# Issuing the loads of x in pieces of three chunks, nine chunks in flight

## The chip, the cores and the metric

One NeuronCore of one Trainium2 chip. TensorE (PE, with its weight loads as PEld), VectorE (DVE), ScalarE (ACT), GpSimd (POOL) and SyncE (SP) each work through a list of instructions of their own; 16 DMA engines move data. The metric is the device time of one execution in microseconds (us), the median of several runs. The kernel before takes 177.07 us, the median of 3 runs from 176.68 to 177.59.

## The reference

x is 8 batches of 4224 tokens of 192 numbers, in float32. It goes through a causal convolution over 7 tokens whose weights are softmax-normalised, one set for each of 8 groups of 24 channels, and the result y through token mixing:

```
w   = softmax(weight, axis=-1)                       # 8 x 7
y   = sum over k of w[h, k] * x_padded[b, s + k, h]  # per group h of 24 channels
wq, wk = y @ w_q, y @ w_k                            # 192 -> 64
W   = (wq @ wk.T) / 8                                # 4224 x 4224, never formed here
out = relu(W @ y) @ w_out
```

The kernel uses (wq @ wk.T) @ y = wq @ (w_k.T @ (y.T @ y)): a Gram matrix y.T @ y of 192 x 192 for each batch, a small matrix M made of it, and then wq @ M for all tokens, relu, and the product with w_out.

## The kernel before

**Tiles.** Tokens are cut into chunks of 122 (CW); with the 6 tokens before them a chunk fills the 128 partitions. A batch has NCC = 35 chunks. XW (line 355) holds all chunks of all 8 batches as bfloat16, so no load of x ever waits for a buffer. The convolution of a group of channels is a product of XW with a banded matrix BAND, line 654.

**Groups.** A batch's chunks are loaded and convolved by groups: four of 9, 9, 9 and 8 chunks in batch 0, two of 18 and 17 chunks in the others (groups_of, line 314).

**Loads.** gen_load (line 535) makes the loads of one group, issued on POOL, which turns float32 into bfloat16 on the way: the first chunk of a batch by itself (it has no tokens before it), all full chunks of the group in one DMA, and the last chunk by itself (82 rows). A batch after batch 0 has four DMAs: 1 and 17 chunks, 16 and 1 chunks. All DMAs of a group count on one semaphore of its own, and the group's convolutions (gen_conv, line 636) wait for it. POOL has nothing else to do after a few microseconds, and no load of x waits for an earlier one. The SP queue issues the loads of the weights and, line 978, the stores of the output, from four buffers (NOUT).

**Stages of a batch.** After a group's convolution (lines 391 and 392 are the helper that records each pair of matmuls) ACT or DVE writes y to SBUF (line 671). PE transposes y (lines 395, 396 and 726) and multiplies it with w_q (lines 751 and 755), and adds up the Gram matrix (line 787). From it come M (lines 806 to 860), the mixing (lines 878 and 890), relu (lines 907 and 908), the product with w_out (line 935 and the helper at 391 and 392), its copy to the output buffer (line 970) and the store. The mixing of a batch is interleaved with the convolutions, transposes and Gram matmuls of the next.

**The order.** Each operation is an Op with an estimated duration, the operations it needs, and a priority vt. Planner.plan (line 143) places them one by one on the engines, by readiness and then by vt, and so writes each engine's list before anything runs. The priorities are read one after another from the list TURNS (line 13), one entry for each operation in the order in which they are made:

```
op.vt = TURNS[len(planner.ops)]
```

For a load the planner does not use the time at which its issue ends alone but a due time, `op.lands`, which counts 260 ns for each chunk loaded so far. Program.place (line 232) then turns each operation's needs into semaphore waits. A wait is left out where the engine, or the clock of another operation waited for, already vouches for it:

```
for source in list(waits):
    if any(s != source and waits[s][2].get(source, 0) >= waits[source][0] for s in waits):
        del waits[source]
```

A wait that an instruction doesn't carry itself is an instruction of its own on the engine (line 269).

Of the kernel before, what the change touches and what calls it, by code (L numbers as in the profile page):

```python
# [12 lines left out]
TURNS = [  # L13
    int(t) / 1000
    for t in """
# [56 lines left out]
class Op:  # L72


    n = 0
# [199 lines left out]


Op.dma = None


def bass_lightweight_conv__then__hypermixer_token_mlp_kernel(  # L280
# [8 lines left out]
    B, S, D = x.shape  # L289
    H, KC = weight.shape  # L290
# [5 lines left out]
    x_t, out_t, w_t = x.tensor, out.tensor, weight.tensor  # L296
    wq_t, wk_t, wo_t = moe_w_q.tensor, moe_w_k.tensor, moe_w_out.tensor

    CW = 128 - (KC - 1)
# [7 lines left out]
    while t < S:  # L307
        n = 512 if S - t >= 1024 else 128
# [5 lines left out]
    def groups_of(b):  # L314
        size = 9 if b == 0 else 18
        return [list(range(c, min(c + size, NCC))) for c in range(0, NCC, size)]
# [4 lines left out]
    def sbuf(name, shape, dtype):  # L321
        return es.enter_context(nc.sbuf_tensor(name, shape, dtype))

    def semaphore(name):
        return es.enter_context(nc.semaphore(name))
# [29 lines left out]
    XW = sbuf("xw", [128, B, NCC, D], BF16)  # L355
# [16 lines left out]
    planner = Planner(nbank=7, first_bank=0)  # L372
# [1 line left out]
    def bank(i, n=1):  # L374
        return PS[:, i * 512 : (i + n) * 512]

    def add(*a, dma=None, kind=None, **k):
        op = Op(*a, **k)
        op.dma = dma
        op.kind = kind  # L380
        op.vt = TURNS[len(planner.ops)]
        return planner.add(op)

    def evac_ns(cols, fast=1):
# [9 lines left out]
    def turn_halves(e, out, in_, identity):  # L394
# [3 lines left out]

    S_W = semaphore("s_w")
    load_w = add(  # L400
        "SP",
        lambda e, op: e.dma_start(WT_F[:, :, :], bass.AP(w_t, 0, [[0, 128], [1, H * KC]])),
        100,
        dma=("w", S_W, 16),
        tail=2500,
        vt=-9,
    )

    one = add("DVE", lambda e, op: e.memset(IDENT[:, :], 1.0), 100, vt=-9.5)
    zero_w = add("DVE", lambda e, op: e.memset(WQT[64:128, :, wq_cols[-2] :], 0.0), 150, vt=-8.51)  # L410
    zero_yt = add("DVE", lambda e, op: e.memset(YTH[64:128, wq_cols[-2] :], 0.0), 100, vt=-8.52)
    zero_s = add("DVE", lambda e, op: e.memset(STEPT[:, :], 0.0), 150, vt=-8.9)
# [18 lines left out]
        vt=-9,  # L431
# [99 lines left out]

    load = {}
    at = [5000.0]

    def gen_load(b, gi):
        sem = semaphore(f"s_x{b}_{gi}")
        cs = groups_of(b)[gi]
        parts = []
        base = b * S * D
        full = [c for c in cs if 0 < c < NCC - 1]  # L540
        if cs[0] == 0:
            parts.append((XW[KC - 1 : 128, b, 0, :], bass.AP(x_t, base, [[D, CW], [1, D]])))
        n = len(full)
        parts.append(
            (
                XW[:, b, full[0] : full[0] + n, :],
                bass.AP(x_t, base + (CW * full[0] - KC + 1) * D, [[D, 128], [CW * D, n], [1, D]]),
            )
        )
        if cs[-1] == NCC - 1:  # L550
            rows = S - (CW * (NCC - 1) - KC + 1)
            parts.append(
                (
                    XW[0:rows, b, NCC - 1, :],
                    bass.AP(x_t, base + (CW * (NCC - 1) - KC + 1) * D, [[D, rows], [1, D]]),
                )
            )

        at[0] += len(cs) * 260.0
        load[b, gi] = []  # L560
        for k, part in enumerate(parts):
            first = (b, gi) == (0, 0) and part[0].shape[1] > 1 and len(part[0].shape) == 3
            op = add(
                "POOL",
                lambda e, op, part=part: e.dma_start(*part),  # L565
                900,
                needs=[zero_x] if cs[-1] == NCC - 1 else [],
                after=[] if first else [ident],
                dma=(f"x{b}_{gi}", sem, 16),
                vt=-10 if first else -4 + b + gi * 0.1 + 0.02 * k,  # L570
            )
            op.tail = 1500.0
            op.lands = at[0]
            load[b, gi].append(op)

    for gi in range(len(groups_of(0))):
        gen_load(0, gi)
# [40 lines left out]
    for b in range(1, B):  # L618
        for gi in range(len(groups_of(b))):
            gen_load(b, gi)  # L620
# [386 lines left out]
        later = nxt  # L1007

    planner.plan()

    program = Program(semaphore)
    for op in planner.order:
# [46 lines left out]
```

## Time and profile before

| what | us |
|---|---|
| median of 3 runs | 177.07 |
| the profiled execution: span from its first to its last instruction | 175.7 |
| PE busy | 157.1 |
| ACT busy | 123.5 |
| DVE busy | 118.0 |
| POOL busy | 30.3 |

The profiled execution is a run of its own; its span lies 1.4 us below the median of the runs. In the view of the DMA queues, q0 are the loads that POOL issues, q1 those and the stores that SP issues, and q8 the engines' instructions. The sizes there are those of the written side: a chunk of x is 48 KB as bfloat16 and twice that as it is read. In the windows, each engine has its busy time and in brackets its number of instructions, then come the granted TensorE clock as a share, the DMA engines' share (over 1 where transfers overlap) and GB/s.

Where in the span the loads and the convolutions stood, from the issue and landing rows of the loads and the timeline of PE:

| batch and group | last load of the group landed, us | its first convolution, us |
|---|---|---|
| 1, first | 21.3 | 23.5 |
| 1, second | 25.6 | 28.6 |
| 2, first | 30.2 | 34.4 |
| 2, second | 34.5 | 37.8 |
| 3, first | 39.1 | 47.7 |
| 3, second | 45.5 | 54.4 |
| 7, second | 106.0 | 134.0 |

### The profile page before, as it was taken

The page shows a single profiled execution, that of the slowest core. Times are in us where ns is not written, and L with a number is a line of the kernel's source. Part 1 is how long each engine was busy: PE and PEld are TensorE (multiplying, and loading weights), DVE is VectorE, ACT ScalarE, POOL GpSimd, SP SyncE. Part 2 cuts the span into 40 slices and gives each one's busy share as a digit, 9 for nine tenths or more (in the row PEclk, how much of TensorE's full clock was granted, in tenths as well). Part 3 has the DMA queues.
Part 4 walks back from the last instruction along what each step waited for, and adds up shares of the span by engine and source line. Part 5 has one row for each costly group of instructions (what it writes and reads, how often), then busy time and mean ns, then how long its engine had stood idle before and what let it go on. Part 6 is the DMA issues. An engine that isn't in the chain of part 4 may idle for free.

```text
span 175.7 us, 7099 instructions
## 1 busy us (share of the span) xinstructions
PE 157.1 (89%) x3226; PEld 121.7 (69%) x3226; DVE 118.0 (67%) x216; ACT 123.5 (70%) x206; POOL 30.3 (17%) x39
## 2 busy tenths in 40 slices
PE   0289799888999999899989979999999999999990
PEld 0179666776787787668778766878767777877550
DVE  6556587765766677586787738689688675765740
ACT  3243677597787948668648747888888896698980
POOL 7999452524230000000000000000000000000000
PEclk9999999999999999999999999999999999999995
DMA  3999999999999999999999999067283045987787
GB/s 30 162 189 186 205 191 193 191 196 277 193 279 194 286 309 268 343 250 243 304 264 282 237 194 348 24 244 297 103 343 127 4 175 216 356 347 309 265 303 262
DMA packets 48157, 40.36 MB, mean 230 GB/s; under 512 B 37632, under 2 KB 40960, under 8 KB 48128
## 3 DMA queue, kind: packets, MB, share of 16 engines
q0 software_dynamic: 36128, 13.61, 65.1%
q1 hardware_dynamic: 12000, 26.31, 40.9%
q8 instruction: 25, 0.41, 0.9%
q14 instruction: 4, 0.03, 0.1%
HBM read 27.56 MB, written 25.95 MB: 305 GB/s over the span
## 4 chain that ended last, share of the span: by engine, by line
PE 88%; issue 4%; DVE 3%; ACT 2%
PE ps L391 25%; PE ps L787 14%; PE ps L935 8%; PE ps L392 7%; PE ps L395 6%; PE ps L726 6%; PE ps L878 5%; PE ps L751 4%; PE ps L890 4%; PE ps L755 4%; PE ps L396 3%; ACT rt L907 1%; ACT out_sb L970 1%; DVE band L527 0%; DVE xw L416 0%
## 5 line engine op out<-in xcount | busy, mean ns | idle before, releaser
L970 ACT COPY out_sb<-ps 128x768 f32<-128x768 f32 (+1 forms) x46 | 34.7, 768 | 15.1 <-PE ps L392 11.3
L671 ACT CAST y<-ps 122x816 bf16<-122x816 f32 (+3 forms) x46 | 35.7, 791 | 13.2 <-PE ps L392 12.8
L907 ACT ACTIVATE rt<-ps 128x1024 bf16<-128x1024 f32 (+3 forms) x44 | 34.1, 800 | 6.4 <-PE ps L878 4.5
L787 PE MATMUL ps<-y 122*64 122x192 bf16 (+4 forms) x840 | 33.8, 222 | 2.2 <-issue 2.2
L970 DVE COPY out_sb<-ps 128x768 f32<-128x768 f32 (+1 forms) x26 | 21.6, 840 | 19.7 <-PE ps L392 18.5
L392 PE MATMUL ps<-wol,rt 128*64 128x192 bf16 x264 | 33.9, 255 | 1.0 <-issue 1.0
L787 PEld LDWEIGHTS ps<-y 122*64 122x64 bf16 (+1 forms) x840 | 31.1, 112 | 4.9 <-issue 2.8
L565 POOL DMA_DIRECT2D xw<-in_x_dram x34 | 29.9, 893 | 22.3 <-issue 21.5
L391 PE MATMUL ps<-wol,rt 128*64 128x192 bf16 x264 | 33.7, 255 | 0.0
L391 PE MATMUL ps<-xw,band 128*64 128x432 bf16 (+3 forms) x144 | 31.8, 335 | 1.5 <-DVE band L527 0.9
L392 PE MATMUL ps<-xw,band 128*64 128x432 bf16 (+3 forms) x144 | 32.1, 337 | 1.1 <-issue 1.1
L391 PEld LDWEIGHTS ps<-wol,rt 128*64 128x64 bf16 x264 | 24.1, 138 | 8.1 <-issue 2.0
L908 DVE TENSOR_SCALAR rt<-ps 128x512 bf16<-128x512 f32 (+3 forms) x36 | 23.6, 674 | 8.2 <-PE ps L878 7.6
L671 DVE CAST y<-ps 122x864 bf16<-122x864 f32 (+3 forms) x26 | 23.6, 912 | 8.0 <-PE ps L392 7.5
L698 DVE COPY ytl<-ps 128x976 bf16<-128x976 bf16 (+1 forms) x40 | 23.0, 591 | 3.9 <-PE ps L396 3.3
L392 PEld LDWEIGHTS ps<-wol,rt 128*64 128x64 bf16 x264 | 24.1, 138 | 1.2 <-issue 1.2
L396 PE MATMUL ps<-ident,y 122*64 122x122 bf16 x280 | 21.1, 219 | 0.0
L395 PE MATMUL ps<-ident,y 122*64 122x122 bf16 x280 | 21.0, 219 | 0.0
L935 PE MATMUL ps<-woh,rt 64*128 64x192 bf16 x264 | 20.4, 250 | 0.2 <-ACT rt L907 0.2
L395 PEld LDWEIGHTS ps<-ident,y 122*64 122x64 bf16 x280 | 18.1, 112 | 2.0 <-issue 0.5
L726 PE MATMUL ps<-ident,y 122*64 122x122 bf16 (+1 forms) x344 | 17.1, 220 | 1.3 <-DVE y L671 0.7
L396 PEld LDWEIGHTS ps<-ident,y 122*64 122x64 bf16 x280 | 17.7, 112 | 0.0
(95 smaller groups left out, 218.8 us busy)
## 6 DMA issues: line engine op xcount, KB each, us to landing
out_dram<-out_sb SPq DMA_DIRECT2D x28, 768.0 KB, 5.1
xw<-in_x_dram POOLq DMA_DIRECT2D x7, 816.0 KB, 33.2
xw<-in_x_dram POOLq DMA_DIRECT2D x7, 768.0 KB, 33.7
out_dram<-out_sb SPq DMA_DIRECT2D x8, 384.0 KB, 3.3
xw<-in_x_dram POOLq DMA_DIRECT2D x2, 432.0 KB, 8.3
out_dram<-out_sb SPq DMA_DIRECT2D x8, 96.0 KB, 4.3
xw<-in_x_dram POOLq DMA_DIRECT2D x1, 384.0 KB, 5.2
xw<-in_x_dram POOLq DMA_DIRECT2D x8, 45.8 KB, 25.0
```

The lines of the kernel that those rows point to most:

```text
L391: e.matmul(out[0:64], lhsT[:, 0:64], rhs, **k)
L392: return e.matmul(out[64:128], lhsT[:, 64:128], rhs, **k)
L395: e.transpose(out[0:64], in_[:, 0:64], identity)
L396: return e.transpose(out[64:128], in_[:, 64:128], identity)
L565: lambda e, op, part=part: e.dma_start(*part),
L671: return e.copy(dst, src) if op.engine == "ACT" else e.tensor_copy(dst, src)
L726: last = e.transpose(ps[64 * i : 64 * i + HI, o : o + w], Y[0:w, yb, c, LO:D], IDENT[0:w, 0:w])
L787: mm = e.matmul(bank(GB)[p : p + 64, o : o + z - r], Y[0:w, yb, c, r : r + 64], Y[0:w, yb, c, r:z], start=st, stop=end, skip_group_check=True,
L907: return e.activation(dst, src(), AF.Relu)
L908: return e.tensor_scalar(dst, src(), 0.0, None, op0=ALU.max)
L935: last = e.matmul(bank(op.bank + a)[:, o : o + D], RT[64 * a : 64 * a + HI, slot, 2, i:n:nt], WOH[64 * a : 64 * a + HI, :], start=i == q, ...
L970: return e.copy(dst, src) if op.engine == "ACT" else e.tensor_copy(dst, src)
```

## The change

From batch 1 on, the full chunks of a group are no longer one DMA but pieces of at most three chunks: 3, 3, 3, 3, 3, 2 in a batch's first group and 3, 3, 3, 3, 3, 1 in its second. With the first and last chunk these are 14 DMAs in a batch where there were four, 98 where there were 28. Batch 0 is loaded as before.

The pieces take turns on six semaphores, and each gets a gate: going back from a piece, itself included, the chunks are added up, and the piece at which the sum first exceeds nine has to have landed before this one is issued. POOL waits for that. The convolutions of a group now need all its pieces, on several semaphores.

The gates are added after planning, so that the planner does not see them. A group's pieces share the estimated 900 ns of the one DMA, and all have its priority: TURNS is now read by an iterator, and pieces after the first of a group take over the priority of the operation made just before.

```diff
+    turns = iter(TURNS)
+
-    def add(*a, dma=None, kind=None, **k):
+    def add(*a, dma=None, kind=None, again=False, **k):
         op = Op(*a, **k)
         op.dma = dma
         op.kind = kind
-        op.vt = TURNS[len(planner.ops)]
+        op.vt = planner.ops[-1].vt if again else next(turns)
         return planner.add(op)
...
+    NFLY, AHEAD = 6, 9
+    S_X = [semaphore(f"s_x{i}") for i in range(NFLY)]
+    pieces_of_x = []
...
-        sem = semaphore(f"s_x{b}_{gi}")
+        sem = semaphore(f"s_x{b}_{gi}") if b == 0 else None
...
-        n = len(full)
-        parts.append(
-            (
-                XW[:, b, full[0] : full[0] + n, :],
-                bass.AP(x_t, base + (CW * full[0] - KC + 1) * D, [[D, 128], [CW * D, n], [1, D]]),
+        lead = len(parts)
+        piece = len(full) if b == 0 else 3
+        for f in range(0, len(full), piece):
+            n = min(piece, len(full) - f)
+            parts.append(
+                (
+                    XW[:, b, full[f] : full[f] + n, :],
+                    bass.AP(x_t, base + (CW * full[f] - KC + 1) * D, [[D, 128], [CW * D, n], [1, D]]),
+                )
             )
-        )
...
-                900,
+                900 / -(-len(full) // piece) if lead <= k < lead + -(-len(full) // piece) else 900,
...
-                dma=(f"x{b}_{gi}", sem, 16),
-                vt=-10 if first else -4 + b + gi * 0.1 + 0.02 * k,
+                dma=(f"x{b}_{gi}", sem, 16) if b == 0 else None,
+                again=lead < k < lead + -(-len(full) // piece),
             )
...
+            if b > 0:
+                i = len(pieces_of_x)
+                op.dma = (f"x{i % NFLY}", S_X[i % NFLY], 16)
+                chunks = part[0].shape[1] if len(part[0].shape) == 3 else 1
+                pieces_of_x.append((op, chunks))
+                flying = 0
+                for j in range(i, -1, -1):
+                    flying += pieces_of_x[j][1]
+                    if flying > AHEAD:
+                        assert i - j < NFLY
+                        op.gate = pieces_of_x[j][0]
+                        break
...
     planner.plan()
+    for op, _ in pieces_of_x:
+        if op.gate is not None:
+            op.needs.append(op.gate)
```

More of the change, by code (lines that the diff above doesn't have):

```diff
@@ L277 @@
 Op.dma = None
+Op.gate = None
 def bass_lightweight_conv__then__hypermixer_token_mlp_kernel(
```

## The prediction

> **What bounds the kernel now.** First the page: the engines' busy times, the DMA slices, the DMA queues and the chain that ended last.
>
> ```profile
> span 175.7 us, 7099 instructions
> ...
> PE 157.1 (89%) x3226; PEld 121.7 (69%) x3226; DVE 118.0 (67%) x216; ACT 123.5 (70%) x206; POOL 30.3 (17%) x39
> ...
> DMA  3999999999999999999999999067283045987787
> ...
> q0 software_dynamic: 36128, 13.61, 65.1%
> q1 hardware_dynamic: 12000, 26.31, 40.9%
> q8 instruction: 25, 0.41, 0.9%
> ...
> PE 88%; issue 4%; DVE 3%; ACT 2%
> ```
>
> PE carries 88% of the chain, so the end moves with what PE waits for. The loads of x (q0) fill the DMA engines up to slice 25, about 110 us; after that only stores run. The chain has 4% "issue", time in which PE waited for nothing that the profile shows. The view of all waits says where:
>
> ```profile
> PE ps L787 <- issue: 2.2, 2, 1.3
> PE ps L392 <- issue: 2.1, 2, 1.1
> ...
> PE ps L391 <- issue: 0.6, 1, 0.6
> PE ps L726 <- issue: 0.5, 1, 0.5
> ```
>
> Six waits, 5.4 us. The chain and PE's timeline give their starts: 19.2 (1.28 us), 32.6 (0.50), 39.1 (1.07), 70.1 (0.90), 89.6 (0.59), 102.1 (0.99), 5.33 us together. None falls after the loads have ended. Narrowing the view of the DMA queues to 0.2 us around each finds a q8 transfer that began 1.2 to 2 us before it (18.0, 30.8, 37.7, 68.7, 87.8, 100.7). The 25 transfers of q8, 0.41 MB, are 16 KB each, and PE's 6452 matmuls and weight loads are 258 to each: PE's own program, some 128 matmuls a block. How far PE had got when a block's transfer began is read from the count of matmuls (PE's x) in windows from 0 to that time, here blocks 2, 4, 16 and 20:
>
> ```profile
> 0.00:24.40 24.40, 15.04 (x318) 13.72 (x320) 14.59 (x43) 10.01 (x25) 20.22 (x28) 1.00 1.31 158
> ...
> 0.00:37.70 37.70, 27.75 (x574) 23.18 (x576) 23.97 (x58) 20.17 (x40) 25.04 (x33) 1.00 1.42 171
> ...
> 0.00:109.50 109.50, 96.01 (x2006) 76.45 (x2006) 74.71 (x144) 71.32 (x124) 30.31 (x39) 1.00 1.36 233
> ...
> 0.00:134.40 134.40, 120.91 (x2524) 95.56 (x2526) 94.31 (x175) 91.99 (x156) 30.31 (x39) 1.00 1.20 226
> ```
>
> Less 128 a block that is +62 and +62 while loads run, -42 and -36 after. A block starts about 100 matmuls later under the loads, over 5 us at 54 ns each (175.7/3226). So I read the six waits as PE's program arriving late behind queued loads.
>
> **Part 1, the queue in front of the program.** Before, POOL runs far ahead: a 17-chunk load takes a median of 33.2 us from issue to landing. After, at most nine chunks are outstanding, 2.3 us of transfer at 0.255 us a chunk (48 KB at the 192 GB/s of 21 to 24 us). A delay of 5 us cannot come from 2.3 us of queue, but the loads still run, and beside stores a turn is longer. Bounds: nothing gained, or all 5.33 us. I take three quarters, 4.0 us: 1.3 of the 1.78 before 37.8 us, 2.7 of the 3.55 after it, passed on in full since the chain is PE.
>
> The Trainium skill says otherwise ("Runtime: NRT & Kernel Launch", Instruction fetch mechanics): the next 16 KB block is fetched while one executes, and crossing a block is "mostly hidden". The blocks agree in size; six of the 14 fetches that begin before 104 us are not hidden. By the rule this part would be worth nothing.
>
> **Part 2, POOL.** 28 loads of batches 1 to 7 become 98: per batch ten of three chunks, one of two, three of one. The rows for POOL's issuing and for a landing:
>
> ```profile
> L565 POOL DMA_DIRECT2D xw<-in_x_dram x34: 545/984/1338, 1.3 to 52.5; - x34
> ...
> xw<-in_x_dram POOLq DMA_DIRECT2D x1, 384.0 KB, 5.2
> ...
> xw<-in_x_dram POOLq DMA_DIRECT2D x1, 30.8 KB, 21.3
> ```
>
> One chunk takes 0.55 us of POOL, seven 0.98; three lie between, 0.70 by the straight line. A batch costs 10 x 0.70 + 0.62 + 3 x 0.55 = 9.3 us where it cost 3.6 (1.29 + 1.18 + 2 x 0.55): 40 us more over seven batches. I cost it at nothing: POOL has nothing but loads after 2.6 us, so what waits behind a gate is only the next piece, and the convolutions take a batch about every 16 us. If that cover is gone, it shows in part 3.
>
> **Part 3, the slower loads.** A piece is issued when the piece some nine chunks earlier has landed, so the rate is what is in flight (7 to 9 chunks, 8.2 on average over the pattern) per round trip. No load of before went out into a short queue while others were streaming. Nearest is the very first, 384 KB or eight chunks, 5.2 us: less five chunks (1.3) and 0.3 of issuing that is 3.6 us, the slow end, because its DMA engines started cold (46 GB/s in the fourth microsecond, 181 in the next two). The fast end is 0.70 of issuing + 0.77 of data + the 0.7 us that lay between the end of the first issue (2.3) and its first packet (3.0) + an estimated 0.2 for semaphores, 2.4 us. I take 2.8, nearer the fast end, because the stream is warm; the 0.4 is for the slowest of 16 engines.
>
> A rule speaks against the change: the skill's "DMA: Bandwidth & Descriptors", Anatomy of one DMA, fits a GpSimd load as 2.0 us plus its bytes at 436 GB/s; three chunks of float32, 295 KB, would be 2.7 us by that estimate. Batch 2 below would land at 37.0.
>
> The stage that decides is 15 to 38 us. Batch 0 lands at 15.2 (last issue 6.14 + 9.0). The first seven chunks of batch 1 are ungated; 63 more up to the end of batch 2 go at 8.2 per 2.8 us, 21.5 us, and the first trip, behind a drained queue, costs about 1 us: 15.4 + 21.5 + 1.0 = 37.9. Before, they landed at 34.5 (issue 13.20 + 21.3, the row above). Their convolution began here:
>
> ```profile
> 37.81 0.34 PE L391 MATMUL ps<-xw,band 128*64 128x408 bf16 x1
> ```
>
> So that convolution is 0.1 us late, PE having saved 1.3 us by then and losing it here. With 2.4 us the batch lands at 34.6, nothing late; with 3.6 at 44.5, 6.7 us late. PE issues in order, so behind this convolution stand the transposes, Gram and mixing matmuls, and ACT and DVE wait with them. What is late next: batch 3's second group, 8.8 us in hand before (54.35 against 45.5), and 35 chunks more at 12.0 us a batch land at 49.9, in time. From batch 4 on the margins were 15 to 30 us, more than the some 10 us by which the loads stretch.
>
> **Part 4, semaphores.** A convolution group waited for one semaphore; now for the pieces that no gate vouches for, three in the first group, four in the second. That is five more waits a batch, 35 in all.
>
> ```profile
> L269 PEldq EVENT_SEMAPHORE  x46: 51/51/51, 8.7 to 168.7; - x46
> ```
>
> 35 x 51 ns = 1.8 us bare; the 46 of now lie under matmuls of 190 to 390 ns. Bounds 0 and 1.8; I take 0.4. Planned order, evacuations and stores stay: planned landings (from the kernel's own due times) do not move with the pieces. Stores have less queue beside them (7 to 8 us to landing at 40 to 100 us, 4.3 after 110), but one wait in the whole view is for a store, 2.4 us of ACT, so I put that at nothing; lost, it would cost those 2.4 us again.
>
> **Sum.** -2.7 (fetches after 37.8) + 0.1 (up to it) + 0.4 = -2.2 us on a span of 175.7. The runs' median, 177.07, is 1.4 us above the span, so 174.9.
>
> **Rivals.** (a) The gate starves PE early. Place: the convolution at 37.8 us; price 63/8.2 = 7.7 us for each microsecond of round trip; with 3.6 us, 6.7 - 2.7 + 0.4 = +4.4, time 181.5. It decides from 3.1 us on, where 2.3 us of lateness eat the gain. For: a margin of 3.3 us, no row with a warm short trip, the slowest engine rules each gate. Against: the stream is warm, and ungated pieces follow each other without a dip (193 GB/s at 24 to 25.5 us across three boundaries).
> (b) Depth does not matter for the fetches. If the engines take turns between queues, a fetch waits for one turn of q0 however long its queue, and the delay stays while loads run. Then 0.1 is lost by 37.8 (the 1.78 still stands in PE's way), plus 0.4: 177.6. For: in eight of 14 fetches the same queue caused no stall. Against: smaller pieces may make the turns shorter too. The DMA page of the skill (Queues, rings and completion order) states such turns, packet by packet; by that rule this rival holds.
> (c) All stalls go and the trip is 2.4 us: -5.33 + 0.4 = -4.9, time 172.2.
>
> **Chances.** Forecast 0.38, (a) 0.28, (b) 0.22, (c) 0.12. What a measurement tells from no change is about 0.5%, 0.9 us. The forecast's own range is 173.5 to 176.3, nearly all faster; (a) begins at 3.1 us with "same" and is mostly slower; (b) is mostly same, partly slower. Faster 0.38 x 0.92 + 0.12 = 0.47; slower 0.28 x 0.85 + 0.22 x 0.4 = 0.33; same 0.20. The range takes in (b), nearly all of (c) and most of (a): 172.3 to 181.0.
>
> **What would show it.** Part 1: no wait for "issue" of over 0.5 us on PE, and counts at block starts 40 or more matmuls lower. Part 2: 104 loads, the last landing between 115 and 122 us. Part 3: three-chunk pieces landing 2.4 to 3.1 us after issue around 20 to 35 us, and a wait of PE for xw near 36 to 38 us of about 1.4 us. Part 4: some 80 semaphore instructions on PE, no gaps beside them. It is wrong if the trips are longer than 3.1 us, if the six waits stay, or if a later group of convolutions waits for its load.

## The result and the profile after

| | before | after |
|---|---|---|
| median of the runs, us | 177.33 (176.68 to 178.83, 4 runs) | 209.53 (207.84 to 211.49, 4 runs) |
| span of the profiled execution, us | 175.7 | 209.7 |
| PE busy, us | 157.1 | 166.7 |
| PE waiting for loads of x, us | 0 | 29.7 |
| PE's waits for "issue", us | 5.4 | 0.4 |

The profiled execution is the slowest of the four, 211.49 us, and counts as a slow one: the ratio, 1.1764 with a 95% interval of 1.1687 to 1.1841, goes by the other three (207.84 to 209.66). The forecast was 174.9, the range 172.3 to 181.0: wrong in direction and far outside. These are the lines of the page of the changed kernel that answer to those shown of before; line 574 is now the issue of the loads, and 394 and 395 are the helper's lines.

```profile
span 209.7 us, 7183 instructions
...
PE 166.7 (79%) x3226; PEld 127.0 (61%) x3226; DVE 118.1 (56%) x216; ACT 124.5 (59%) x206; POOL 75.5 (36%) x109
...
PEclk9999996996799999699999699999999669999999
DMA  4999999999998999999999999999999302688788
...
DMA 67%; PE 17%; POOL 7%; issue 5%; ACT 2%; POOLq 0%
```

PE's 88% of the chain has become 17%, and 67% is one thing: a load of x that the next load was waiting for. The chain's 5% of "issue" are POOL's, mostly some 0.3 us between a landing and the next issue; PE's own are the 0.4 us of the table. The loads run on into slice 32, to about 165.5 us (the last is issued at 163.5 and takes 2.1 us), where they ended at 106. The row PEclk has dips that it did not have before:

```profile
PEclk9999999999999999999999999999999999999995
```

The view of all waits names both ends of the chain:

```profile
POOL xw L574 <- DMA xw<-in_x_dram: 81.9, 59, 6.5
...
PE ps L394 <- DMA xw<-in_x_dram: 29.7, 9, 6.2
```

POOL stands 81.9 us at the gates, and PE nine times, 29.7 us, before a group's first convolution. The timeline of PE has these nine; the number in brackets is the wait. Here are the last of batch 2, of batch 4 and of batch 7, and the first of batch 4:

```profile
49.34 0.55 PE L394 MATMUL ps<-xw,band 128*64 128x408 bf16 x1 [5.78 <-DMA xw<-in_x_dram]
...
85.23 0.37 PE L394 MATMUL ps<-xw,band 128*64 128x432 bf16 x1 [3.84 <-DMA xw<-in_x_dram]
...
94.40 0.36 PE L394 MATMUL ps<-xw,band 128*64 128x408 bf16 x1 [3.01 <-DMA xw<-in_x_dram]
...
165.59 0.55 PE L394 MATMUL ps<-xw,band 128*64 128x408 bf16 x1 [6.16 <-DMA xw<-in_x_dram]
```

The first is the convolution on which the prediction staked its sum: expected at 37.9 us, it began at 49.3. By then four waits (1.59, 2.65, 2.10, 5.78) cost 12.1 us; the other five, 17.6 us, come later, up to batch 7, where the prediction saw no danger at all.

A wait costs more than its length. Windows behind the wait that ended at 49.34 (the first number in brackets is PE's matmuls, the one before the DMA share the granted clock):

```profile
49.40:55.00 5.60, 5.60 (x61) 3.68 (x63) 1.77 (x4) 2.52 (x3) 2.43 (x4) 0.50 1.14 117
55.10:60.70 5.60, 5.60 (x114) 4.25 (x111) 3.93 (x10) 4.75 (x7) 3.65 (x5) 1.00 0.91 93
```

PE is busy all through the first 5.6 us and gets 61 matmuls done at a granted clock of 0.50; in the next 5.6 us it does 114. There are five such stretches with a clock of 0.50, about 31.2 to 34.6, 48.3 to 55.1, 85.8 to 89.3, 116.6 to 120.0 and 164.3 to 171.2 us, each at the end of a wait of 2.65 us or more; PE works in some 22 of these 24 us, at half its clock.

The bill: 29.7 us of waits, 9.6 us more of PE's busy time (166.7 - 157.1), less 5.0 us of waiting for "issue", 34.3 in all; the spans differ by 34.0.

### The profile page after: what moved, and what is told of

It reads as the page before. It is cut to its first block, busy times and chain, and to the rows that moved or that the text cites. A ratio compares the mean times of both kernels' runs of the same rounds, so it can differ in the third digit from the quotient of the medians.

```text
span 209.7 us, 7183 instructions
## 1 busy us (share of the span) xinstructions
PE 166.7 (79%) x3226; PEld 127.0 (61%) x3226; DVE 118.1 (56%) x216; ACT 124.5 (59%) x206; POOL 75.5 (36%) x109
## 4 chain that ended last, share of the span: by engine, by line
DMA 67%; PE 17%; POOL 7%; issue 5%; ACT 2%; POOLq 0%
DMA xw<-in_x_dram 67%; POOL xw L574 7%; PE ps L394 6%; PE ps L956 3%; PE ps L808 2%; PE ps L398 2%; PE ps L899 2%; PE ps L911 1%; ACT rt L928 1%; PE ps L772 1%; ACT out_sb L991 1%; PE ps L747 1%; PE ps L776 1%; PE ps L395 0%; PE ps L399 0%
## 5 line engine op out<-in xcount | busy, mean ns | idle before, releaser
L574 POOL DMA_DIRECT2D xw<-in_x_dram x104 | 75.1, 725 | 88.1 <-DMA xw<-in_x_dram 81.9
L394 PE MATMUL ps<-xw,band 128*64 128x432 bf16 (+3 forms) x144 | 36.9, 376 | 30.6 <-DMA xw<-in_x_dram 29.7
L395 PE MATMUL ps<-xw,band 128*64 128x432 bf16 (+3 forms) x144 | 36.9, 377 | 0.0
L394 PEld LDWEIGHTS ps<-xw,band 128*64 128x64 bf16 x144 | 15.3, 127 | 35.7 <-DMA xw<-in_x_dram 31.7
L808 PE MATMUL ps<-y 122*64 122x192 bf16 (+3 forms) x840 | 35.9, 231 | 0.4 <-issue 0.4
L808 PEld LDWEIGHTS ps<-y 122*64 122x64 bf16 x840 | 33.4, 118 | 3.7 <-issue 1.7
L929 DVE TENSOR_SCALAR rt<-ps 128x512 bf16<-128x512 f32 (+3 forms) x36 | 23.7, 674 | 12.1 <-PE ps L899 9.0
L399 PE MATMUL ps<-ident,y 122*64 122x122 bf16 x280 | 22.0, 225 | 0.0
L398 PE MATMUL ps<-ident,y 122*64 122x122 bf16 x280 | 22.0, 225 | 0.0
L398 PEld LDWEIGHTS ps<-ident,y 122*64 122x64 bf16 x280 | 19.0, 116 | 2.4 <-issue 1.1
L399 PEld LDWEIGHTS ps<-ident,y 122*64 122x64 bf16 x280 | 18.7, 116 | 0.2
```

The costliest lines, as they stand in the source:

```text
L394: e.matmul(out[0:64], lhsT[:, 0:64], rhs, **k)
L395: return e.matmul(out[64:128], lhsT[:, 64:128], rhs, **k)
L398: e.transpose(out[0:64], in_[:, 0:64], identity)
L399: return e.transpose(out[64:128], in_[:, 64:128], identity)
L808: mm = e.matmul(bank(GB)[p : p + 64, o : o + z - r], Y[0:w, yb, c, r : r + 64], Y[0:w, yb, c, r:z], start=st, stop=end, skip_group_check=True,
L929: return e.tensor_scalar(dst, src(), 0.0, None, op0=ALU.max)
```

## The experiments

Each time stands beside runs of the kernel before on the same chip (177.34 to 177.80 us). "G" in the expectations is the theory that the gate's round trip sets the rate of the loads.

**Pieces without gates, and a deeper gate.** The first run keeps the pieces and drops the gates; a group's pieces share one semaphore, as its loads did before.

```diff
-        sem = semaphore(f"s_x{b}_{gi}") if b == 0 else None
+        sem = semaphore(f"s_x{b}_{gi}")
...
-                dma=(f"x{b}_{gi}", sem, 16) if b == 0 else None,
+                dma=(f"x{b}_{gi}", sem, 16),
...
-            if b > 0:
-                i = len(pieces_of_x)
...
```

> Pieces of three chunks as in the change, but no gate: POOL issues them as fast as it can, each group on one semaphore. Theory G (the loss is the gate's round trip: eight chunks in flight per 4 us and more): no wait of PE for xw, no half clock in the middle of the run, time 172 to 178 us, near the kernel before. Rival P (small DMAs are themselves slow, by their issue on POOL or by overhead at each piece): loads still take 17 us or more a batch, PE waits for xw, time over 195 us. On the program fetches: if the size of a piece sets how long a fetch waits, PE's waits for issue shrink below 1 us in total; if the depth of the queue sets it, they stay near 5 us.

178.0 us against 177.8, ratio 1.0013 (0.9998 to 1.0027): the pieces cost nothing that can be told. POOL spends the same 75 us on 104 loads as in the changed kernel (75.1 against 75.5 busy), but ahead of need. PE's waits for "issue" in this run:

```profile
PE ps L395 <- issue: 2.3, 3, 1.1
...
PE ps L796 <- issue: 1.5, 2, 0.9
...
PE ps L394 <- issue: 0.6, 1, 0.6
...
PE ps L735 <- issue: 0.5, 1, 0.5
...
PE ps L944 <- issue: 0.5, 1, 0.5
```

That is 5.4 us of "issue", as before: smaller pieces alone do not bring PE's program earlier.

```diff
-    NFLY, AHEAD = 6, 9
+    NFLY, AHEAD = 12, 18
```

> The change with 18 chunks in flight instead of nine (12 semaphores). Theory G: with a fixed part of some 3 us in a round trip and 0.255 us a chunk, 16 to 17 chunks per 7.2 us or less is nearly the full rate, some 9 to 11 us a batch before the stores begin; PE waits for xw at most 4 us in total; time 171 to 181 us. Rival P: as slow as with nine, over 195 us.

175.16, 180.22, 180.59 and 181.81 us. The timeline of PE in the profiled execution (span 178.8) has one wait for x, at the second group of batch 2:

```profile
40.74 0.35 PE L394 MATMUL ps<-xw,band 128*64 128x408 bf16 x1 [3.46 <-DMA xw<-in_x_dram]
```

There is a dip of the clock behind it, and 3.4 us of "issue" in the whole run. So 18 chunks nearly suffice. The four times lie too far apart for a verdict, and whether the execution of 175.16 us did without that wait was not seen.

```diff
-    NFLY, AHEAD = 6, 9
+    NFLY, AHEAD = 20, 36
```

> The change with 36 chunks in flight (20 semaphores). Theory G: full rate, no wait of PE for xw, time 170 to 178 us. Rival P: over 195 us. If the depth of the queue sets how late PE's program arrives, its waits for issue lie between those of 18 in flight and those of the kernel before.

178.37 us, ratio 1.0043 (1.0023 to 1.0064): no wait for x, but 5.9 us of "issue" and no gain. The last expectation was missed: 5.9 does not lie between the 3.4 with 18 in flight and the 5.4 of before.

```diff
-    NFLY, AHEAD = 6, 9
+    NFLY, AHEAD = 16, 24
```

> 24 chunks in flight, between 18, where one execution took 175.2 us and three some 180, and 36, 178.4. Theory G: 24 chunks are 6.1 us of transfer, more than the trips of 3.1 to 6.5 us seen with 18, so PE does not wait for xw; its program arrives earlier than with 36, waits for issue 3.5 to 5 us: 176 to 178 us. Rival: the order of the transfers is uneven enough that PE still waits at 38 to 41 us in some executions: 178 to 181 us.

178.21 us, ratio 1.0049 (1.0016 to 1.0082), single times from 176.12 to 179.32: both expectations partly. The profiled execution, the fastest, has no wait for x and 4.3 us of "issue", a span of 174.3. It was not seen what the longer ones spend their time on.

**The gate without the pieces.**

```diff
-    NFLY, AHEAD = 6, 9
+    NFLY, AHEAD = 6, 18
...
-        piece = len(full) if b == 0 else 3
+        piece = len(full)
```

> The gate without the pieces: the full chunks of a group in one DMA as before, at most 18 chunks in flight, which leaves one large DMA at a time. Theory G: about 7.5 us a trip (the first load's 5.2 us for eight chunks, eight more chunks at 0.255, 0.28 to wake POOL), 15 us a batch; the second group of batch 2 lands near 44 us, PE waits for xw 5 us or more in all, time 181 to 195 us although no piece is small. Rival P: no small DMAs, so 175 to 178 us.

214.02 us, one run. The direction is as G has it although no load is cut into pieces (a batch's first and last chunk were small DMAs before, too), but the size was missed: 195 us was the upper end. The rows of its loads and POOL's timeline:

```profile
xw<-in_x_dram POOLq DMA_DIRECT2D x7, 816.0 KB, 9.2
xw<-in_x_dram POOLq DMA_DIRECT2D x7, 768.0 KB, 9.5
```

```profile
29.93 1.28 POOL L574 DMA_DIRECT2D xw<-in_x_dram  x1 [6.16 <-DMA xw<-in_x_dram]
39.41 2.25 POOL L574 DMA_DIRECT2D xw<-in_x_dram  x3 [8.19 <-DMA xw<-in_x_dram]
```

A group takes 9.2 us to land where I had reckoned 7.2, so a batch takes 18 to 19 us of loads instead of 15.

**What a lone piece takes.** One piece at a time.

```diff
-    NFLY, AHEAD = 6, 9
+    NFLY, AHEAD = 6, 3
```

> The change with three chunks in flight, one piece at a time, so that the trip of a lone piece can be read. If the prediction's 2.8 us was right and the change's 3.7 us and more came from the three pieces sharing the DMA engines, a lone piece lands 2.2 to 2.6 us after its issue where no stores run. If the fixed part was undersized, it lands 3 us or more after it even alone. The kernel is load-bound: 98 trips of 2.5 to 4 us, 280 to 420 us.

387.72 us. POOL's timeline before the stores begin (start, duration, the idle time before it in brackets) and the landing row of the same stretch:

```profile
22.88 0.76 POOL L574 DMA_DIRECT2D xw<-in_x_dram  x1 [2.91 <-DMA xw<-in_x_dram]
26.57 0.76 POOL L574 DMA_DIRECT2D xw<-in_x_dram  x1 [2.93 <-DMA xw<-in_x_dram]
30.04 0.76 POOL L574 DMA_DIRECT2D xw<-in_x_dram  x1 [2.71 <-DMA xw<-in_x_dram]
```

```profile
xw<-in_x_dram POOLq DMA_DIRECT2D x3, 144.0 KB, 3.3
```

The row of GB/s over 22 to 34 us, 40 slices of 0.3 us, shows when the data of three pieces moved:

```profile
GB/s 37 0 0 0 0 0 0 8 46 78 166 150 40 4 0 0 0 0 0 0 64 69 142 156 60 0 0 0 0 0 0 12 50 88 180 146 15 0 0 0
```

One piece follows the other by 3.5 to 3.7 us: 3.3 to landing and some 0.3 until POOL goes on, with nothing else of size on the DMA engines. A piece spreads over five to seven slices; by the windows its packets take 1.45 to 1.67 us, at 88 to 102 GB/s, where a full queue moved 192. The trip of the prediction, 2.8 us, was not to be had.

**Early and late apart.** First the deep queue for batches 1 to 3 and the change's nine from batch 4 on, then the reverse.

```diff
-                    if flying > AHEAD:
+                    if flying > (36 if b < 4 else 9):
```

> 36 chunks in flight for batches 1 to 3, the change's nine only from batch 4 on, where the kernel before had 15 to 30 us in hand. Theory as in the prediction (the loss is in the first three batches; later groups have enough in hand): no wait of PE for xw, 175 to 179 us. Rival S (nine in flight cannot keep pace beside the stores, where a batch takes 22 us of loads and PE needs some 17): waits for xw at batches 5 to 7, half clock behind them, 185 to 200 us.

189.79 us against 177.34: 12.4 us lost where the prediction saw 15 to 30 us in hand. Rival S holds, only that the first of its waits comes a batch earlier than it said. PE's timeline has three waits for x, 11.1 us:

```profile
74.78 0.52 PE L394 MATMUL ps<-xw,band 128*64 128x408 bf16 x1 [2.81 <-DMA xw<-in_x_dram]
...
97.88 0.33 PE L394 MATMUL ps<-xw,band 128*64 128x408 bf16 x1 [3.48 <-DMA xw<-in_x_dram]
...
145.00 0.52 PE L394 MATMUL ps<-xw,band 128*64 128x408 bf16 x1 [4.83 <-DMA xw<-in_x_dram]
```

They are second groups, of batches 4, 5 and 7, and the clock dips to a half behind each.

```diff
+                    if flying > (9 if b < 4 else 36):
```

> The other half of the run with nine in flight from batch 4 on: nine for batches 1 to 3, 36 from batch 4 on. If the loss of the change is the sum of an early part (trips of 4 us before the stores begin) and a late part (longer trips beside the stores, 12.4 us by the run from batch 4 on), the waits for xw up to 60 us stay at about 12 us in total with half clock behind the longest, none come after, and the kernel loses 10 to 16 us: 187 to 193 us. If the early waits only bring the later ones forward, it loses most of the change's 32 us: over 195 us. The prediction's own price for a trip of 3.6 to 4.1 us, an early loss of 4 to 8 us, would be 181 to 185 us.

197.05 us against 177.66: 19.4 us: past the additive expectation of 187 to 193, and on the numbers in the band of the rival. The view of all waits has this line for x:

```profile
PE ps L394 <- DMA xw<-in_x_dram: 15.7, 5, 5.4
```

Four of the five, up to 67.3 us, make 11.9 us, as the additive theory had it; the fifth, 3.8 us at 90.3, where that theory had none, is the second group of batch 4, whose loads are issued behind the late ones. PE is busy 5.9 us longer than before (163.0). The two halves, 12.4 and 19.4, make 31.8 us; the whole change loses 32.2. So on these numbers, two executions of each half, the parts add up after all, and what I had too low was the early one: its waits, its clock and the wait behind it.

**What a single wait costs.** The kernel before, whose convolutions of batch 4's first group also wait for a load that lands later.

```diff
     planner.plan()
+    for cb, cg, mm in convs:
+        if (cb, cg) == (4, 0):
+            mm.needs += load[5, 1]
```

> The kernel before, with one wait added and nothing else: the convolutions of batch 4's first group also wait for the second group of batch 5 (landed at 77.1 us, where they began at 67.9). Theory C (an idle PE loses its clock for a while after): PE waits some 9 us there, the granted clock is about a half for 3.4 to 6.8 us behind it, and the kernel loses 11 to 13 us, more than it waits: 188 to 191 us. Rival (a wait costs its own length, less the waits for issue that it hides): 183 to 187 us and no half clock.

185.47 us, ratio 1.0454 (1.0400 to 1.0508), 8.1 us more; the wait was 8.73 us. Windows behind it:

```profile
76.90:80.60 3.70, 3.70 (x34) 2.41 (x34) 1.34 (x2) 2.06 (x3) 0.00 (x0) 0.50 1.60 193
80.80:84.50 3.70, 3.70 (x69) 2.74 (x70) 2.59 (x5) 2.72 (x4) 0.00 (x0) 1.00 1.60 192
```

The half clock is there without any change to the loads: 34 matmuls against 69 in the same time, a loss of nearly 2 us (PE busy 158.7, 1.6 more). The total fell in the rival's range all the same, because the waits for "issue" shrank from 5.4 to 3.0 us. So the theory had the clock right and the sum wrong. The queue of loads in this run is as deep as before: one wait of PE was enough to take 2.4 us off its waits for "issue".

**A version meant to beat both.** If a short queue helps PE's program and landings cost trips, the loads may be paced by PE: whole groups, each issued when the convolution three groups earlier (or two) has begun.

```diff
     planner.plan()
+    for g in range(3, len(groups)):
+        begun = min(convs[groups[g - 3]], key=lambda op: at_of[op.id])
+        for k, op in enumerate(load[groups[g]]):
+            op.needs.append(begun)
+            key[op.id] = at_of[begun.id] + 0.1 * (k + 1)
+    planner.order.sort(key=lambda op: key[op.id])
```

> The loads of before, whole, with another gate: a group's loads are issued when the convolution three groups earlier has begun on PE, so no load waits for a landing. Theory: the queue is short after the first 45 us and there is no round trip between loads, so PE never waits for xw, and its waits for issue after 45 us (2.5 us before) go below 1 us: 174 to 176.5 us. Rival (the queue is still deep whenever a group of 17 chunks stands in it): waits for issue as before, 177 to 178 us.

178.49 us, ratio 1.0021 (0.9984 to 1.0058), no wait for x, 4.3 us of "issue": the theory's 174 to 176.5 us was missed.

> As the one before with two groups instead of three. Theory: waits for issue lower still, also before 45 us, but the second group of batch 2 is issued at 28.6 us and lands at 36 to 39, where PE needs it at 37.8: 173.5 to 177 us if it comes in time, 177 to 180 if PE waits for it.

178.45 us, ratio 1.0005 (0.9975 to 1.0036), with 2 in place of 3 in the edit: 2.4 us of "issue", but 1.9 us of waits for x at batch 2. Then 36 in flight early and 18 later:

```diff
+                    if flying > (36 if b < 3 else 18):
```

> 36 chunks in flight for batches 1 and 2, 18 from batch 3 on. Theory G: the only place at which 18 ran dry was the second group of batch 2, near 41 us, so PE does not wait for xw any more; the waits for issue up to 40 us come back (2 to 2.8 us), those after shrink: 175.5 to 177.5 us. Rival (18 runs dry later as well, beside the stores): 179 us and more, with waits for xw at later groups.

173.87, 177.05, 177.47 and 177.81 us beside 177.34. The profiled execution (177.47) has no wait for x, as the theory had it, but its waits for "issue" did not shrink: 5.4 us. What the one of 173.87 did differently was not seen. No version is shown to beat the kernel before.

## Why the prediction was wrong, point by point

**Part 3, the slower loads, failed, three times over.** First its duration. The page of before had one load that went out into an empty queue, 5.2 us, which works out at 3.6 us for three chunks. I set it aside as a cold start and took 2.8, a sum of parts. In the run with a lone piece, 3.6 us was the plain trip, and the parts show where the sum was short. The issue, 0.76 us, and the 0.7 us from its end to the first packet came as reckoned. The data, 0.77 us and 0.4 more for the slowest engine, took 1.45 to 1.67: 0.77 is what three chunks take in a full queue, and why a lone piece moves more slowly stays open. From the last packet to POOL's next issue it took some 0.6 us (0.3 to the landing, 0.3 until POOL went on) where 0.2 was reckoned. With three pieces on the way the trip was longer, as the landing row of line 574 in the changed kernel over 20 to 36 us shows, median 3.7 of all pieces, and 3.8 of those of three chunks:

```profile
DMA to landing us min/median/max: 2.5/3.7/4.6
```

By the prediction's own formula a trip of 4.1 us, 3.8 and 0.3 until POOL goes on, gives 15.4 + 63 x 4.1/8.2 + 1.0 = 47.9 us for the end of batch 2; its convolution began at 49.3. The formula was nearly right and its main term mis-sized. (With 3.6 us it gives 44.1, not the 44.5 of the prediction.) The Trainium skill ("DMA: Bandwidth & Descriptors", Anatomy of one DMA) would give an estimated 2.7 us for this piece; the measured 3.3 to its landing decides.

Second, the margins of 15 to 30 us from batch 4 on. I compared them with a delay, "some 10 us", when what counts is the rate. Where the stores run, the trips were longer; this row of the DMA view over 65 to 140 us has the pieces of three, with 5.2 us where it was 3.8:

```profile
xw<-in_x_dram POOLq DMA_DIRECT2D x33, 144.0 KB, 5.2
```

Releases of PE at 67.8, 94.4 and 116.6 us, the second groups of batches 3, 4 and 5, lie 27 and 22 us apart; in the kernel before these convolutions began at 54.35, 73.46 and 92.17 us, some 19 apart. A margin is used up by such a difference in a few batches; the run with nine in flight from batch 4 on lost 12.4 us by that and the clock behind its waits. POOL's 9.3 us a batch, which I weighed against some 16, was not what limited it: the same pieces without gates cost nothing.

Third, a term that was not in the sum: PE's clock after a wait. The granted clock was 0.50 in five stretches here, and the run with one added wait shows that a wait alone brings such a stretch on. The 9.6 us that it cost are more than a quarter of the loss, and rival (a) should have carried them. The Trainium skill's "TensorE: Matmul & The Clock Gate", Part 1, has it: the array runs at half speed after an idle window of about 3.4 us, until it has been busy for as long. The stretches here, about 3.4 or 6.8 us long, agree with that; the wait of 2.65 us that was enough is shorter than the page's window, and there the measurement decides.

**Part 1, the queue in front of the program, came out in direction, but its cause is not shown.** The waits for "issue" went from 5.4 to 0.4 us, more than the 4.0 reckoned. Less 128 matmuls a block, as in the prediction, PE's lead when a block's transfer began, averaged over the blocks that began while loads ran:

| chunks in flight | matmuls beyond 128 a block | waits for "issue", us |
|---|---|---|
| unlimited, whole groups (before) | 42 | 5.4 |
| unlimited, pieces of three | 42 | 5.4 |
| 36 | 36 | 5.9 |
| 24 | 33 | 4.3 |
| 18 | 10 | 3.4 |
| 9 (the change) | -11 | 0.4 |

Two of the windows behind the last row, up to 0.1 us after the starts of blocks 3 and 10 (388 - 384 = 4 and 1224 - 1280 = -56):

```profile
0.00:28.20 28.20, 18.50 (x388) 15.39 (x388) 17.75 (x49) 13.03 (x32) 14.94 (x24) 1.00 1.11 129
...
0.00:87.50 87.50, 62.88 (x1224) 49.34 (x1226) 46.87 (x96) 45.45 (x80) 42.89 (x63) 0.93 1.06 161
```

The size of a piece makes no difference to the blocks. With less in flight they begin earlier, but the waits for "issue" go down by more than 1.1 us only where PE waits for x as well, and its program can arrive in that time. The profiled executions without a wait for x, however deep the queue, have 4.3 to 5.9 us of "issue", the one with 36 and then 18 in flight 5.4; the run with one added wait and the queue of before has 3.0. So how much of the fall to 0.4 us is due to the short queue stays open, the direction may have come out by luck, and rival (b) is not refuted. What failed is that the gain could be had: at depths where the loads keep pace, little of the 5.4 us goes. The prediction also read too much from its two blocks at +62: they are among the highest of 15 (average 42), and the ten after the loads average -23, so that a block began some 65 matmuls later under the loads, 3.5 us, and not 100.

**Part 2** was right: 0.76 us for a piece of three chunks where 0.70 was reckoned, and POOL's 75 us are hidden, as the run without gates shows; the last landing, 165.5 us instead of 115 to 122, is the fault of part 3. **Part 4** fits: PE has 60 semaphore instructions, not some 80, against 46, and the bill above leaves nothing for them; no run tested them alone.

**Rival (a)** named the mechanism, the place and the point from which it decides, 3.1 us. It had 0.28 of the chances and a time of 181.5, priced as a single late convolution; the first four waits, the five after them and the clock made it 209.5.

## What to carry to other kernels

A limit on what is in flight that is released by landings is a rate: chunks in flight over the trip, and the trip includes the issue, the landing and the wake of the issuing engine, here 3.6 us alone for a piece that a full queue moves in 0.8 us. Take the trip from a load that went out into an empty queue, and compare the rate with what the consumer needs in every stage, busiest DMA stage included; a margin in time says nothing where the rate is too low. And price a long wait of TensorE with the half clock behind it. Before a shorter queue is credited with a gain, see whether the engine that gained was also made to wait.

## What the runs showed of the hardware

- The DMA view's digits do not tell a saturated stream from a starved one: from 24 to 30 us the changed kernel moved 112 GB/s at a DMA share of 1.03, the pieces without gates 190 GB/s at 1.59, and the digits are nines in both.
- A wait of 2.65 us (to 30.9) was enough for half clock from 31.2 on, one of 3.01 us (to 94.4) was not. With the runs of 18 in flight and of nine for a part of the batches taken in, the other waits for x of 2.81 us and more were all followed by it, and none of 2.16 us or less.
- Small DMAs issued ahead cost nothing that can be told here: 98 loads in place of 28, ratio 1.0013 (0.9998 to 1.0027).
- A lone piece of three chunks moved at 88 to 102 GB/s, a full queue at 192: a transfer's time in a full queue is not its time alone.
